# Order of the row gathers behind a router: the tiles of 128 of experts 0 and 1 ahead of the gathers of later experts

## The chip, the cores and the metric

One core of a Trainium2 chip. The metric is the time of one execution on the device in microseconds, as the median of several runs.

## The reference

Three stages run one after the other on 1536 tokens of width 512: an attention with a local window and block summaries, a layer of 8 experts of which each token uses at most one, and a dense network with a cosine. Only the second is touched by the change:

```python
skip_score = x @ w_skip
do_compute = skip_score > 0
xc = x[do_compute]
logits = xc @ w_gate
e_idx = np.argmax(logits, axis=1)
...
for e in range(E):                      # 8 experts, w1[e]: 512x1024, w2[e]: 1024x512
    mask = e_idx == e
    h = np.maximum(xc[mask] @ w1[e], 0.0)
    y[mask] = gate_w[mask, None] * (h @ w2[e])
out[do_compute] = xc + y
```

The third stage is `g = h * cos(h)` with `h = x @ w_in`, and `g @ w_out` (512 to 2048 and back).

## The kernel before, in words

**Stages.** The attention ends at about 85 us of the span and leaves all rows in a DRAM tensor xb. The router counts the tokens of each expert (CNT) and makes lists of row numbers: GIA for the first 32 tokens of each expert (64 half rows), GIS for up to 64 more, GIB for a full tile of 128 more. Which of the last two is used depends on the count: up to 32 tokens neither, up to 96 the 64 rows, above that the 128 rows (with the 64 again for what is left in some cases). The branches are real ones, evaluated by every engine from registers (`tc.If`, L941, L1169, L1171, L1173).

**Gathers.** Three helpers issue an indirect DMA each from GpSimd (all through L626): `ex_gather(e)` fetches the first rows of expert e into xg (e = 2 to 7; those of 0 and 1 are issued earlier, at L817 and L818), `ov_gather(e)` the 64 rows into xo, and `many_gather(e)` the 128 rows into xm, if the count asks for it. `many_gather` first loads two counts into registers on every engine. GpSimd issues in program order.

**The expert loop** (L1261 on). For expert e TensorE turns the hidden rows of e (`ex_t`), multiplies the rows of expert e + 1 with its first matrix (`ex_w1`, L642), turns the rows of expert e + 2 (`ex_x`, L604), and multiplies with the second matrix of e (`ex_w2`, L979). `ex_out` adds and scatters the rows (L630); a scatter into xb waits for the gathers that read xb before it. `overflow(e)` then turns the 64 rows (L995, 64x64), and if there are more, the 128 rows xm (L995, 128x128), and multiplies them with both matrices (`full_tile`, L1034, L1049, result at L1059). Between these the tables `WORK` and `START` put work of the next stage: conversions of w_in and w_out (raw loads L897, then L907 to L920) and the order of rows (L1065 on).

**Weights.** `load_piece` (L179) issues 512 KB of an expert's matrices from SyncE (SP); four pieces are one matrix, a unit, and eight units have buffers at a time. A piece waits for the gather that is handed to it (`after`), otherwise for the landing of the piece three ahead of it (`AHEAD`). Units 4 (expert 2's first matrix) and before are loaded during the attention; the pieces that the changed lines pace are those of units 5, 6 and 7, twelve in all. Units 8 to 15 are asked for at the end of each of the first four experts, when the buffers of that expert come free. SP also works in program order.

**The third stage** begins at about 223 us. It is a row of matmuls on TensorE (L1188, L1333, L1399), with the conversions beside them, and ends with scatters to the output.

Of the kernel before, what the change touches and what calls it, by code (L numbers as in the profile page):

```python
# [31 lines left out]
NE = 8  # L32
# [83 lines left out]
def tile_kernel(ctx: ExitStack, tc: tile.TileContext, consts, qh, kh, vh, vw, w9, w1, w2, w_in, w_out, out):  # L116
# [56 lines left out]
    def load_w(u):  # L173
        pool = ring[u % NU]
        wt[u] = pool.tile([P, 4096], F32, tag="w", name="w")
        for part in range(4):
            wq.append((u, part))

    def load_piece(after=None, half=None):  # L179

        if not wq:
            return
        u, part = wq.pop(0) if half != 0 else wq[0]
        e, kind = divmod(u, 2)
        k, w = (4, w1) if kind == 0 else (8, w2)
        ks, fs = slice(part * k // 4, (part + 1) * k // 4), slice(None)
        if half is not None and kind == 0:
            fs = slice(512 * half, 512 * half + 512)
        elif half is not None:
            ks = slice(2 * part + half, 2 * part + half + 1)  # L190
        d = nc.sync.dma_start(out=wt[u].rearrange("p (k f) -> p k f", k=k)[:, ks, fs],
                              in_=w[e].rearrange("(k p) f -> p k f", p=P)[:, ks, fs])
        if after is None and len(pieces) >= AHEAD:
            after = pieces[-AHEAD]
        if after is not None:
            tc.add_manual_dep(d.ins, after.ins.name, SYNC, reason="pace")
        pieces.append(d)
# [427 lines left out]
    def gather(dst, idx, src):  # L625
        return nc.gpsimd.indirect_dma_start(out=dst, out_offset=None, in_=src,  # L626
                                            in_offset=bass.IndirectOffsetOnAxis(ap=idx, axis=0))
# [10 lines left out]
    def ex_w1(e, ph, h):  # L638
        w, x = W1(e), xe.pop(e)
        for k in range(4):  # L640
            for c in range(4):
                nc.tensor.matmul(ph[CAP * c:CAP * c + CAP, :], x[:, QA * (k % 2) + CAP * (k // 2):][:, 0:CAP],  # L642
                                 w[:, k, 256 * c:256 * c + 256],
                                 start=(k == 0), stop=(k == 3), skip_group_check=True)
        nc.scalar.activation(out=h, in_=ph, func=AF.Relu)
        hs[e] = h
# [234 lines left out]
    def cv_alloc(q, half):  # L881
        if q == 2:
            WQ[q, half] = WQ[0, half]
        else:
            t = (wpb if q % 2 else wpa).tile([P, 2, 4, 512], F32R, tag="w", name="wx")
            WQ[q, half] = (t[:, 0], t[:, 1])
# [3 lines left out]
    def cv_load(q, i, after=None):  # L890
        kind, j = divmod(i, 4)
        r = cvt.tile([P, 1024], I32, tag="raw", name="raw", bufs=3 if q == 0 else 2)
        if kind == 0:
            src = w_in[j * P:(j + 1) * P, q * 512:(q + 1) * 512].bitcast(I32)
        else:
            src = w_out[(4 * q + j) * P:(4 * q + j + 1) * P, :].bitcast(I32)
        d = nc.sync.dma_start(out=r, in_=src)  # L897
        if after is not None:
            tc.add_manual_dep(d.ins, after.ins.name, SYNC, reason="rows first")
        raws[q, i] = r  # L900
# [23 lines left out]
    def ex_gather(e):  # L924
        xg.append(m1.tile([QA, 256], F32, name=f"xg{e}"))
        return gather(xg[e], GIA[:, e:e + 1], xb2)

    def ov_gather(e):

        xo[e] = ysrc[e] if e < 3 else xo[e - 1] if e == NE - 1 else m1.tile([P, DM], F32, name=f"xo{e}")  # L930
        return gather(half(e), GIS[:, e:e + 1], xb)

    def half(e):
        return xo[e][YT:P] if e == NE - 1 else xo[e][0:YT]
# [3 lines left out]
    def many_gather(e):  # L938
        cnts[e] = cnt(0, e, NTOK), nc.values_load(CNT[0:1, 2, e:e + 1], min_val=0, max_val=1, skip_runtime_bounds_check_because=why)
        xm[e] = m2.tile([P, DM], F32, tag="xm", name="xm")  # L940
        with tc.If(cnts[e][0] > CAP + YT):  # L941
            apart(gather(xm[e], GIB[:, e:e + 1], xb), None, ("m", e % 2))

    def ex_x(e):
        xe[e] = m2.tile([P, P], F32, tag="xe", name="xe")
        turn_x(xg[e], xe[e], ps_g, "g", nc.scalar.copy)
# [4 lines left out]
    def apart(d, to=None, key=None):  # L951

        for p, k in outs + inner:
            if key is None or k != key:
                tc.declare_no_dep(d.ins, p.ins, reason="every token has one slot of one expert")
        if to is not None:
            to.append((d, key))
        return d
# [4 lines left out]
    def ex_t(e):  # L963
        h = hs[e]
        pt = ps_l.tile([P, 2, P], F32, tag="p", name="pth")
        for s in range(2):
            nc.tensor.transpose(pt[:, s, :], h[:, s * P:(s + 1) * P], ident)
        hT = m2.tile([P, 2, P], F32, tag="hT", name="hT")
        nc.scalar.copy(out=hT, in_=pt)
        hs[e] = hT  # L970

    def ex_w2(e, hT, po, ns=range(8)):

        w = W2(e)
        for n in ns:
            c, s = divmod(n, 2)
            for a in range(2):
                o = QA * s + CAP * a
                nc.tensor.matmul(po[o:o + CAP, :], hT[:, s, CAP * c:CAP * c + CAP], w[:, n, 256 * a:256 * a + 256],  # L979
                                 start=(c == 0), stop=(c == 3), skip_group_check=True)  # L980

    def ex_out(e, po, yo=None):
        x = xg[e]
        if yo is None:
            yo = x
        for s in range(2):
            nc.vector.scalar_tensor_tensor(out=yo, in0=po[QA * s:QA * s + QA, :], scalar=GTA[:, e:e + 1], in1=yo if s else x,
                                           op0=ALU.mult, op1=ALU.add)
        d = scatter(xb2, SIA[:, e:e + 1], yo, 2 * NTOK)
        apart(d, outs, ("g", e))  # L990
# [134 lines left out]
    def cnt(k, e, top):  # L1125
        return nc.values_load(CNT[0:1, k, e:e + 1], min_val=0, max_val=top, skip_runtime_bounds_check_because=why)
# [38 lines left out]
    def overflow(e):  # L1165

        x, xb_ = xm.pop(e), half(e)
        n, part = cnts.pop(e)
        with tc.If(n > CAP):  # L1169
            xx = tile_x(xb_, YT, nc.vector.tensor_copy, YT if e == NE - 1 else 0)  # L1170
            with tc.If(n > CAP + YT):  # L1171
                full_tile(W1(e), W2(e), x, GTB[:, e:e + 1], SIB[:, e:e + 1], ("m", e % 2))
            with tc.If(part > 0):  # L1173
                part_tile(e, xb_, xx, GTS[:, e:e + 1], SIS[:, e:e + 1], ("o", e))
# [64 lines left out]
    def do(where, e):  # L1239
        for a in WORK.get(where + str(e), "").split():  # L1240
            kind = a.rstrip("0123456789")
            for i in a[len(kind):] or "0":
                acts[kind](int(i))
# [3 lines left out]
    load_w(7)  # L1247
    cv_load(0, 0, first_in)
    load_piece(first_in)
    for e in range(NE):  # L1250
        if e + 2 < NE:
            load_piece(ex_gather(e + 2))
        load_piece(ov_gather(e))
        if e == 0:
            many_gather(0)
        if e in (1, 3):
            cv_load(0, (e + 1) // 2)
    while wq:
        load_piece()
    do("S", 0)  # L1260
    for e in range(NE):  # L1261
        ex_t(e)
        do("T", e)
        if e + 1 < NE:
            ex_w1(e + 1, ps_h.tile([P, 256], F32, tag="h", name="ph"), m2.tile([P, 256], F32, tag="h", name="h"))
        if e + 2 < NE:
            ex_x(e + 2)
        do("B", e)
        if e + 1 < NE:
            many_gather(e + 1)  # L1270
        po = ps_o.tile([P, 256], F32, tag="o", name="po")
        ex_w2(e, hs.pop(e), po)
        ex_out(e, po)
        overflow(e)
        do("J", e)
        if e == 4:
            cv_alloc(0, 0)
            t = wpa.tile([P, 2, 4, 512], F32R, tag="w", name="yb")
            Y[0] = (t[:, 0], t[:, 1])
        if e == 5:  # L1280
            gs.append(wpa.tile([P, 2, 4, 512], F32R, tag="w", name="g0"))
            cv_alloc(0, 1)
        do("A", e)
        for u in range(2 * e + NU, min(2 * e + 2 + NU, 2 * NE)):
            load_w(u)
        while wq:
            load_piece()
        do("Z", e)
# [176 lines left out]
```

## Time and profile before

| what | value |
|---|---|
| median of 3 runs | 494.01 us (493.82 to 1119.29) |
| profiled execution | 495.81 us, of which the span from first to last instruction is 494.0 us |
| TensorE matmuls busy | 443.3 us, 90% |
| VectorE, ScalarE, GpSimd busy | 308.3, 213.7, 148.9 us |
| mean granted clock of TensorE | 0.960 |
| transfers | 76.09 MB, 154 GB/s over the span |

The page has one row of the granted clock and of the transfers for 40 equal slices of 12.35 us. It shows the clock at a half in the tenth slice, and 230 to 350 GB/s in the first sixteen slices, up to about 198 us, with little behind them. The share of busy time of an engine is a mean over the three stages, so the stretch of the experts, 85 to 223 us, has to be read by itself.

### The profile page before, as it was taken

How to read it: one execution, taken by the hardware profiler on the slowest of the kernel's cores; microseconds unless marked ns; L12 is line 12 of the kernel's file. 1: busy time of each engine (PE TensorE's matmuls, PEld its weight loads, DVE VectorE, ACT ScalarE, POOL GpSimd, SP SyncE). 2: the span in 40 equal slices, each digit the busy share in tenths (PEclk: the TensorE clock that was granted, in tenths of full speed). 3: DMA queues.
4: the chain of work that ended last, by engine and by line, in shares of the span. 5: the costliest groups of instructions: out<-in, count | busy, mean ns of one | idle time of the engine just before them, and what ended most of it. 6: DMA issues, size and time to landing. Idle time of an engine off the chain costs nothing.

```text
span 494.0 us, 8759 instructions
## 1 busy us (share of the span) xinstructions
PE 443.3 (90%) x3037; PEld 331.9 (67%) x3037; DVE 308.3 (62%) x862; ACT 213.7 (43%) x518; POOL 148.9 (30%) x156
## 2 busy tenths in 40 slices
PE   6999998950999886948999999999999999999994
PEld 3878886520444342526888888888888888888883
DVE  4798998640051141465658797999889965563741
ACT  2988885100231130332646566644536433150600
POOL 3576652372120026125115232223123200003033
PEclk9999999985899998997999999999999999999997
DMA  9998986779979897103501322322132000002021
GB/s 238 300 306 294 341 300 235 230 248 304 350 255 317 308 325 278 57 12 100 181 23 47 124 85 86 126 86 88 55 116 85 1 1 0 1 0 75 12 104 67
DMA packets 36785, 76.09 MB, mean 154 GB/s; under 512 B 4249, under 2 KB 12955, under 8 KB 36724
## 3 DMA queue, kind: packets, MB, share of 16 engines
q1 hardware_dynamic: 33476, 66.07, 41.2%
q0 software_dynamic: 3248, 9.27, 5.6%
q8 instruction: 31, 0.51, 0.4%
q14 instruction: 30, 0.25, 0.2%
HBM read 68.15 MB, written 7.60 MB: 153 GB/s over the span
## 4 chain that ended last, share of the span: by engine, by line
PE 29%; issue 18%; DVE 3%; POOL 3%; POOLq 0%; ACT 0%; DVEq 0%; ACTq 0%
PE pf L1188 15%; PE py L1333 11%; POOL out L630 2%; PE py L1399 2%; DVE g L1204 1%; PE pt L1118 1%; DVE cvu L911 0%; DVE cvc L912 0%; DVE u L1194 0%; DVE c L1198 0%; POOL wx L920 0%; POOLq L1461 0%; DVE nn L1193 0%; DVE cvu L909 0%; ACT u L1192 0%
## 5 line engine op out<-in xcount | busy, mean ns | idle before, releaser
L1188 PE MATMUL pf<-yb,wx 128*128 128x512 f32 x576 | 136.3, 394 | 6.6 <-DVEq L1157 4.8
L1188 PEld LDWEIGHTS pf<-yb,wx 128*128 128x128 f32 x576 | 109.1, 190 | 30.4 <-issue 7.8
L1333 PE MATMUL py<-wx,g 128*128 128x512 f32 (+1 forms) x540 | 121.6, 384 | 0.0
L1333 PEld LDWEIGHTS py<-wx,g 128*128 128x128 f32 x540 | 99.9, 188 | 20.2
L1192 ACT ACTIVATE u<-pf,qbias 128x512 f32<-128x512 f32 x46 | 31.5, 684 | 86.7 <-PE pf L1188 82.7
L920 POOL TENSOR_TENSOR wx<-cvc,wx 128x512 fp32r<-128x512 f32 x24 | 34.7, 1445 | 94.7 <-ACT wx L919 91.5
L1204 DVE TENSOR_TENSOR g<-c,g 128x512 fp32r<-128x512 f32 x42 | 42.6, 1015 | 0.8 <-ACT g L1203 0.7
L1339 DVE TENSOR_TENSOR ya<-py,ya 128x512 f32<-128x512 f32 (+1 forms) x37 | 23.8, 671 | 28.2 <-PE py L1333 28.2
L340 ACT ACTIVATE sm<-sm,nm 128x128 f32<-128x128 f32 x96 | 37.5, 393 | 5.6 <-DVE nm L328 5.5
L1193 DVE TENSOR_SCALAR nn<-u 128x512 f32<-128x512 f32 x46 | 19.5, 424 | 30.6 <-ACT u L1192 30.6
L1197 ACT ACTIVATE c<-u 128x512 f32<-128x512 f32 x46 | 28.8, 627 | 17.5 <-DVE g L1204 16.1
L630 POOL DMA_INDIRECT out<-ya,PERM x11 | 10.9, 990 | 79.9 <-DVE ya L1339 79.3
L1194 DVE TENSOR_TENSOR u<-u,nn 128x512 f32<-128x512 f32 x46 | 31.9, 693 | 1.6
L1198 DVE TENSOR_TENSOR c<-pf,c 128x512 f32<-128x512 f32 x46 | 31.5, 684 | 0.9 <-ACT c L1197 0.7
L322 PE MATMUL ps<-kT,qbd 128*128 128x128 f32 x192 | 28.1, 296 | 3.3 <-DMA qbd<-qh 3.3
L350 POOL TENSOR_TENSOR sm<-sm,su 128x512 f32<-128x512 f32 x23 | 23.9, 1040 | 21.5 <-DVE su L349 10.8
L322 PEld LDWEIGHTS ps<-kT,qbd 128*128 128x128 f32 x192 | 26.1, 209 | 4.3 <-issue 4.1
L1203 ACT CAST g<-c 128x512 fp32r<-128x512 f32 x46 | 28.0, 608 | 1.0 <-DVE c L1198 1.0
L1059 DVE SCALAR_TENSOR_TENSOR xm<-pox,GTB,xm 128x512 f32<-128x512 f32 x2 | 1.5, 750 | 42.9 <-PE pox L1049 42.9
L328 DVE CUSTOM_DVE_ANT_0 sm<-ps,cst 128x128 f32<-128x128 f32 x96 | 23.7, 284 | 6.1 <-PE ps L322 6.1
L919 ACT CAST wx<-cvc 128x512 fp32r<-128x512 f32 x24 | 14.9, 622 | 16.4 <-DVE cvc L912 16.4
L979 PE MATMUL po<-w,hT 128*32 128x256 f32 x256 | 18.0, 429 | 3.5 <-ACTq L1169 1.9
(250 smaller groups left out, 631.5 us busy)
## 6 DMA issues: line engine op xcount, KB each, us to landing
w<-w SPq DMA_DIRECT2D x62, 512.0 KB, 5.9
raw<-w_in SPq DMA_DIRECT2D x16, 512.0 KB, 3.9
raw<-w_out SPq DMA_DIRECT2D x16, 512.0 KB, 3.3
kT<-kh SPq DMA_DIRECT2D x8, 384.0 KB, 6.5
vn<-vh SPq DMA_DIRECT2D x12, 256.0 KB, 5.2
xb<-xtok SPq DMA_DIRECT2D x12, 256.0 KB, 4.3
qd<-qh SPq DMA_DIRECT2D x4, 512.0 KB, 5.2
vt<-vw SPq DMA_DIRECT2D x12, 128.0 KB, 4.8
```

Source lines behind the costliest of these rows:

```text
L322: nc.tensor.matmul(ps[:, p, :], q[:, p, :, :].rearrange("p h (a t) -> p (h a) t", t=2)[:, :, t % 2], kT[b][:, p, k0:k0 + P], start=True, s ...
L340: nc.scalar.activation(out=sm[:, p, :], in_=sm[:, p, :], func=AF.Exp, scale=-1.0, bias=nm[:, p:p + 1], accum_out=su[:, p:p + 1])
L350: nc.gpsimd.tensor_tensor(out=sm, in0=sm, in1=su.unsqueeze(2).to_broadcast([P, NP, P]), op=ALU.mult)
L920: eng.tensor_tensor(out=lo, in0=c, in1=hi.bitcast(F32), op=ALU.subtract)
L1188: nc.tensor.matmul(p, w[:, k, fs], y[:, k, :], start=(n == 0), stop=(n == 11))
L1192: nc.scalar.activation(out=u, in_=p, func=AF.Identity, scale=1.0 / (2.0 * math.pi), bias=qbias)
L1194: nc.vector.tensor_tensor(out=u, in0=u, in1=nn, op=ALU.subtract)
L1197: nc.scalar.activation(out=c, in_=u, func=AF.Sin, scale=TWO_PI)
L1198: nc.vector.tensor_tensor(out=c, in0=p, in1=c, op=ALU.mult)
L1203: nc.scalar.copy(out=gh, in_=g)
L1204: (nc.gpsimd if i in POOL_G else nc.vector).tensor_tensor(out=gl, in0=g, in1=gh.bitcast(F32), op=ALU.subtract)
L1333: nc.tensor.matmul(p, a[:, ws], b[:, f, cs], start=(n == 0), stop=(n == 11))
```

## The change

The loop that issues the gathers is written in another order, and the call for the 128 rows of expert 1 moves from the expert loop to it. Nothing is added or left out.

```diff
     load_w(6)
     load_w(7)
     cv_load(0, 0, first_in)
     load_piece(first_in)
-    for e in range(NE):
-        if e + 2 < NE:
-            load_piece(ex_gather(e + 2))
+    for e in range(2, 5):
+        load_piece(ex_gather(e))
+    for e in range(2):
+        many_gather(e)
         load_piece(ov_gather(e))
-        if e == 0:
-            many_gather(0)
-        if e in (1, 3):
-            cv_load(0, (e + 1) // 2)
+    for e in range(2, NE):
+        if e + 3 < NE:
+            load_piece(ex_gather(e + 3))
+        load_piece(ov_gather(e))
+        if e in (3, 5):
+            cv_load(0, (e - 1) // 2)
     while wq:
         load_piece()
...
         do("B", e)
-        if e + 1 < NE:
+        if 0 < e < NE - 1:
             many_gather(e + 1)
```

On GpSimd, before, the gathers behind the routing end like this; xo5 and xo6 are rows of 64 of experts 5 to 7, xm_2049 is the tile of 128 of expert 1, and the scatter is expert 0's result:

```order
L626 DMA xg7_1975<-xb_68,GIA_1006 64x256
L626 DMA xo5_1978<-xb_68,GIS_1010 64x512
L626 DMA xo6_1980<-xb_68,GIS_1010 64x512 x2
L1126 TENSOR_LOAD CNT_83
L939 TENSOR_LOAD CNT_83
L941 COMPARE_AND_BRANCH
L626 DMA xm_2049<-xb_68,GIB_1008 128x512
L941 UNCONDITIONAL_BRANCH
L941 ISA
L941 UNCONDITIONAL_BRANCH
L630 DMA xb_68<-xg0_1691,SIA_1007 3072x256
```

With the change the same queue reads like this from the first xo on; xm_1969 is now the tile of expert 1, and xg3, xg4 and the tile of expert 0 stand ahead of these rows:

```order
L626 DMA xo0_1919<-xb_68,GIS_1010 64x512
L1126 TENSOR_LOAD CNT_83
L939 TENSOR_LOAD CNT_83
L941 COMPARE_AND_BRANCH
L626 DMA xm_1969<-xb_68,GIB_1008 128x512
L941 UNCONDITIONAL_BRANCH
L941 ISA
L941 UNCONDITIONAL_BRANCH
L626 DMA xo1_1920<-xb_68,GIS_1010 64x512
L626 DMA xg5_1974<-xb_68,GIA_1006 64x256
L626 DMA xo2_1921<-xb_68,GIS_1010 64x512
```

The gather of expert 1's 128 rows has moved from the end of the row to the place behind the first xo, and ten gathers follow it now.

On TensorE the register loads and the branch of that gather move from expert 0's second matrix (L979) to a place ahead of the matmul for the order of rows (L1065). These are the two pieces of the difference:

```order
 L941 COMPARE_AND_BRANCH
 L941 UNCONDITIONAL_BRANCH x2
+L1126 TENSOR_LOAD CNT
+L939 TENSOR_LOAD CNT
+L941 COMPARE_AND_BRANCH
+L941 UNCONDITIONAL_BRANCH x2
 L1065 LDWEIGHTS ones
 L1065 MATMUL pd<-ado,ones 128x13
```

The second piece stands 16 matmuls further on, and xg_1927 in it is expert 2's first rows:

```order
 L642 MATMUL ph<-w,cst 32x256 x16
 L604 MATMUL ptx<-ident,xg_1927 128x64 x2
-L1126 TENSOR_LOAD CNT
-L939 TENSOR_LOAD CNT
-L941 COMPARE_AND_BRANCH
-L941 UNCONDITIONAL_BRANCH x2
 L979 MATMUL po<-w,hT 32x256 x16
 L1169 COMPARE_AND_BRANCH
```

The loads of expert 2's gather, which stand at the same place one expert later, stay where they were.

On SyncE the pieces of weights keep their order, and the second and third raw loads move behind pieces of unit 7. The queue now ends like this ahead of the expert loop (128x1024 is a piece of unit 6, 128x2x512 of unit 7):

```order
L191 DMA w<-w 128x1024
L1126 TENSOR_LOAD CNT
L939 TENSOR_LOAD CNT
L941 COMPARE_AND_BRANCH
L941 UNCONDITIONAL_BRANCH x2
L191 DMA w<-w 128x1024 x3
L191 DMA w<-w 128x2x512 x2
L897 DMA raw<-w_in 128x1024
L191 DMA w<-w 128x2x512 x2
L897 DMA raw<-w_in 128x1024
```

Before, one raw load stood ahead of the last three pieces of unit 6 and the other ahead of the last three of unit 7; the pieces are now handed the gathers in the order xg2, xg3, xg4, xo0, xo1, xg5, xo2, xg6, xo3, xg7, xo4.

## Rows read from the trace of the kernel before

**Rows 1.** The chain that ended last, its first piece (start us, us, what).

```profile
222.91 1.19 PE pf L1188 x2
```

**Rows 2.** Engines by stretch: us, busy of PE, PEld, DVE, ACT, POOL, then PEclk, DMA.

```profile
core 0: us, PE busy (x) PEld busy (x) DVE busy (x) ACT busy (x) POOL busy (x), PEclk, DMA share, GB/s
223.00:494.00 271.00, 262.03 (x1172) 216.98 (x1172) 194.04 (x304) 119.66 (x209) 62.29 (x50) 0.98 0.20 67
...
109.00:122.00 13.00, 0.04 (x1) 0.00 (x0) 0.89 (x2) 0.00 (x0) 4.26 (x5) 0.50 0.99 287
...
92.00:104.00 12.00, 9.70 (x162) 5.28 (x158) 7.72 (x44) 2.32 (x7) 4.73 (x6) 1.00 0.63 196
...
140.00:150.00 10.00, 8.85 (x96) 4.56 (x95) 8.14 (x19) 1.50 (x4) 3.70 (x5) 1.00 0.72 239
150.00:166.00 16.00, 16.00 (x51) 6.43 (x49) 0.92 (x2) 2.37 (x4) 1.94 (x2) 1.00 0.94 315
```

**Rows 3.** TensorE in order of time: start, us, instruction, idle time before it and releaser.

```profile
104.31 0.31 PE L604 MATMUL ptx<-ident,xg 64*128 64x64 f32 x2 [2.04 <-DMA xg<-xb,GIA]
105.61 2.82 PE L979 MATMUL po<-w,hT 128*32 128x256 f32 x32 [0.99 <-ACT xe L605]
108.35 0.69 PE L995 MATMUL ptx<-ident,xo 64*128 64x64 f32 x4
122.06 1.09 PE L995 MATMUL ptx<-ident,xm 128*128 128x128 f32 x4 [13.02 <-DMA xm<-xb,GIB]
...
145.97 0.66 PE L995 MATMUL ptx<-ident,xm 128*128 128x128 f32 x4
```

**Rows 4.** GpSimd in order of time, 84 to 132 us.

```profile
97.08 0.90 POOL L626 DMA_INDIRECT xo<-xb,GIS  x1 [5.54 <-DVE GIS L860]
98.95 0.90 POOL L626 DMA_INDIRECT xg<-xb,GIA  x1 [0.97 <-remote]
...
113.52 0.97 POOL L626 DMA_INDIRECT xm<-xb,GIB  x1 [0.30 <-issue]
122.79 0.95 POOL L630 DMA_INDIRECT xb<-xg,SIA  x1 [8.31 <-DMA xm<-xb,GIB]
124.93 0.97 POOL L626 DMA_INDIRECT xm<-xb,GIB  x1 [1.19 <-issue]
```

**Rows 5.** Tiles: xo from 96 to 114 us (first row), then xm in all.

```profile
DMA to landing us min/median/max: 4.4/7.8/8.7
...
L1059 DVE SCALAR_TENSOR_TENSOR xm<-pox,GTB,xm x2: 750/750/751, 140.5 to 162.5; 128x512 f32<-128x512 f32 x2
...
DMA to landing us min/median/max: 3.4/4.6/8.4
```

**Rows 6.** Weight pieces (L191) by window: twelve, eight, eight, sixteen of them.

```profile
L191 SPq DMA_DIRECT2D w<-w x12: 328/372/1602, 93.7 to 116.4; - x12
...
DMA to landing us min/median/max: 3.9/11.5/14.0
...
L191 SPq DMA_DIRECT2D w<-w x8: 328/356/379, 126.8 to 138.3; - x8
...
L191 SPq DMA_DIRECT2D w<-w x8: 328/378/450, 145.4 to 160.1; - x8
...
L191 SPq DMA_DIRECT2D w<-w x16: 328/368/424, 166.1 to 192.1; - x16
```

**Rows 7.** TensorE at experts 5 and 7; DMA queue q8 from 101 to 104.

```profile
182.32 1.91 PE L642 MATMUL ph<-w,xe 128*32 128x256 f32 x27
186.92 0.63 PE L642 MATMUL ph<-w,xe 128*32 128x256 f32 x5 [2.68 <-issue]
...
216.18 1.93 PE L979 MATMUL po<-w,hT 128*32 128x256 f32 x32 [1.89 <-ACTq L1169]
...
q8 instruction: 1, 0.02, 2.2%
```

**Rows 8.** ScalarE in order of time, 122 to 148 us.

```profile
136.76 1.76 ACT L907 ACTIVATE C<-raw 128x512 f32<-128x512 f32 x3
141.75 0.37 ACT L969 COPY hT<-pth 128x256 f32<-128x256 f32 x1 [3.22 <-PE pth L967]
```

## The prediction

> **What bounds the kernel now.** I read three views in this order. First the chain of waits that ended last. It can be followed back no further than 222.91 us, to the first matmul of the second network that has both its operands [rows 1], and from there on TensorE is busy for 262.03 of 271 us [rows 2]. That stretch is more than half of the span, and the change touches none of it: it can only begin sooner. Second the table by stretches of the part before it. [...] Third TensorE's timeline around it: the matmuls that turn the 128 gathered rows of expert 1 (xm) start at 122.06 after 13.02 us of waiting for the gather; a little earlier stand two smaller waits, 2.04 us for the gather of xg3 and 0.99 us ahead of the second matrix of expert 1 [rows 3]. GpSimd's timeline tells why: the gather of xm is issued at 113.52, as the last one of a row of gathers that began at 97.08, one each 1.21 us ((113.52 - 98.95) / 12), and every other gather of that row lands before anything needs it [rows 4]. Expert 0 has no such tile, since there are only two xm gathers; the second, at 124.93, is expert 2's.
>
> **The change, part by part.** The order of work moves on three queues.
>
> *GpSimd.* xg3 and xg4 now follow xg2 at once, in the hole in which GpSimd waits for the indices GIS until 97.08 [rows 4]. They are issued at about 92 and 93 and, with the 4.4 to 8.7 us that gathers took there [rows 5], xg3 lands by 101; TensorE comes to it at 102.3 (104.31 - 2.04), so the 2.04 us go. Behind ov0 (97.08 + 0.90) comes expert 1's xm gather, at about 98.4, and ov1 at 99.7. What lands then, and when? The gathers of 64 rows took 4.4 to 8.7 us, median 7.8, xm took at most 8.4 [rows 5]. So xm is there by 106.8 and ov1 between 104.1 and 108.4; I take the median, 107.5.
>
> *TensorE.* The two register loads and the branch of expert 1's gather move ahead of the matmul of the order of rows. The same three instructions cost 0.99 us at 105.61, where nothing was queued ahead of them [rows 3]; I charge 0.99 at the new place and strike it at 105.61, where the sequencer no longer stops at xg3 and can run ahead. TensorE is then ready for expert 1's rows at 108.35 - 2.04 - 0.99 + 0.99 = 106.3, waits to 107.5 for ov1, and begins on xm 0.7 us later, at 108.2 instead of 122.06. Gain 13.9 us, with bounds of 15.0 (only TensorE decides, 107.0) and 13.0 (ov1 at 8.7).
>
> [...]
>
> *The clock.* The tile of expert 1 took from 122.06 to 140.5, expert 2's from 145.97 to 162.5 [rows 3, 5]: 18.4 against 16.5 us for the same instructions, and the first begins at the half clock that the idle stretch left behind [rows 2]. Without those idle 13 us the clock need not fall. I take 1.5 of these 1.9 us (bounds 0 and 1.9).
>
> *The weights on SyncE.* SP issues in order, and each of twelve pieces (512 KB) waits for one gather. Two of them (those behind xg3 and xg4) now start between 96 and 101 instead of after 104, into 92:104, where the DMA share is only 0.63 [rows 2]. They take 1.05 MB off the full stretch that follows, 3.3 us of it at the 315 GB/s of 150:166 [rows 2]. The row of twelve ended near 130 (116.4 + 13.5, just under the longest landing of 14.0 [rows 6]); now near 126.8. But these two pieces also run beside the xm gather; rival 2 gives what that may cost. [...]
>
> TensorE needs expert 6's first matrix at 182.32 [rows 7], then at about 167.4 (15 us less). From the end of the twelve to it lie 23 transfers of 512 KB: five matrices of four pieces (those of experts 4 and 5 and the first of expert 6) and three raw loads of the second network's weights. At 1.64 us each (eight from 126.8 to 138.3) they are there at 164.5, at 1.73 (sixteen from 166.1 to 192.1) at 166.6 [rows 6]; the gap of 140:150, share 0.72 [rows 2], closes because expert 1's buffers come free sooner. I take 0.5 us of cost. The other end is 2.1 us each, the pace of 145.4 to 160.1 [rows 6], 175.1 and 7.7 us.
>
> *ScalarE and the second xm.* The third raw load now stands behind the twelve pieces, so it lands at about 127. ScalarE comes to these conversions at about 122 (136.76 less 15), and behind them, in its order, stands the copy of hT for expert 2, due at 126.8 (141.75 less 15) [rows 8]: it may be held to 127.5 or a little longer. TensorE's matmuls with expert 3's first matrix, which come before hT is read, cover part of that. I charge 0.5 (0 to 3). Expert 2's xm gather follows the first scatter, which waits for all gathers: the last is now issued at 98.4 + 10 x 1.21 = 110.5, landed by 119.2, the scatter follows, the gather 2.14 us behind that (124.93 - 122.79), and it lands at most 8.4 later, at 130.1 [rows 4, 5]; TensorE wants it at 145.97 - 15 = 131. Nothing.
>
> **The sum.** 13.9 + 1.5 - 0.5 - 0.5 = 14.4 us. The profiled execution took 495.81 with a span of 494.0; it becomes 481.4. The median of the runs is 494.01, 1.8 less than the profiled one, so 479.6. The likeliest case alone ranges from 477.1 (15.0 + 1.9) to 484 (13.0 less 3).
>
> **The rivals.**
> 1. *The weights become the bound.* At 2.1 us a piece expert 6's matrix lands at 175.1, the gain shrinks to 182.32 - 175.1 = 7.2, time 486.8. For it: a DMA share of 0.94 to 0.99 in the full stretches [rows 2]. Against it: the paces of 1.64 and 1.73 before and after that stretch [rows 6]. Chance 0.13.
> 2. *The gather lands late.* With 14.0 us like the slowest weight piece ov1 lands at 113.7, the tile starts at 114.4, 7.7 us sooner, with the clock down as before: 486.3. For it: the pieces moved ahead of it. Against it: no gather took over 8.7, though some ran in the fullest stretch. Chance 0.09.
> 3. *The change doesn't do what it says*: the xm gather, though written earlier, waits for its buffer or indices until near its old time; 494. Its row of before shows only 0.30 us of idle time ahead of it, with no release named, so nothing is known to hold it [rows 4]. Chance 0.05.
> 4. *Slower.* All weights still to come get slower because they now run beside TensorE's work and the gathers without a pause. Expert 7's second matrix is needed at 216.18 [rows 7] and ends 35 transfers after 126.8. From (216.2 - 126.8) / 35 = 2.55 us a piece the whole gain is gone; at 2.8 it lands at 224.8, 8.6 late: 502.6. The slowest pace in the rows is 2.1, and that for eight pieces only [rows 6]. Chance 0.04.
>
> **How the numbers follow.** The forecast has 0.69. Two per cent, about what a measurement of this kernel can tell from no change, is 9.9 us, that is 484.1. Forecast plus the early edges of rivals 1 and 2 (0.03 each, where pace or landing lie half way) make 0.75 for faster; the rest of those two, rival 3 and the mild part of rival 4 make 0.22; slower by over 2% keeps 0.03. The range runs from 476.0, a little under the best bounds, to 488.0, which takes in rivals 1 and 2.
>
> **What would show it.** In the changed profile the matmuls on xm start between 107 and 109 and wait for xo or nothing; GpSimd issues xm near 98.4; the granted clock stays at the upper level through expert 1; the chain's first matmul of the second network moves from 222.9 to about 208.5. If TensorE waits around 165 to 175 for expert 6's weights, rival 1 is right; if xm or ov1 land after 110, rival 2. I am wrong if the stretch from 109 to 122 is still empty, or if the time comes back as waits between 125 and 205.

## The result, and the profile after

The changed kernel took 480.57 us (median of five executions, 479.55 to 482.83) beside 494.01 us for the kernel before: ratio 0.9717, 95% interval 0.9685 to 0.9749. The profiled execution took 482.83 us with a span of 481.0; it is the slowest of the five. That is close to the forecast of 479.6, but the later experiments put a limit on it: in the two later series that ran the same kernel again, on two chips, it took 499 us. Ratios leave out slow executions: of those told of here, 1119.29 us of the kernel before in this measurement and 502.18 us of it in the third series.

First TensorE's timeline of the changed kernel, for the stretch of [rows 3] (start, us, engine, line, instruction, operands, count, idle time before it and what ended it):

```profile
97.53 0.18 PE L1065 MATMUL pd<-ado,ones 128*128 128x13 bf16 x1 [1.51 <-issue]
...
104.39 0.33 PE L604 MATMUL ptx<-ident,xg 64*128 64x64 f32 x2
104.65 1.49 PE L979 MATMUL po<-w,hT 128*32 128x256 f32 x20
108.01 1.06 PE L979 MATMUL po<-w,hT 128*32 128x256 f32 x12 [1.87 <-issue]
110.22 0.54 PE L995 MATMUL ptx<-ident,xo 64*128 64x64 f32 x4 [1.15 <-DVE xg L987]
110.69 1.11 PE L995 MATMUL ptx<-ident,xm 128*128 128x128 f32 x4
...
130.36 0.46 PE L1095 MATMUL ptt<-oi,OR 128*128 128x24 bf16 x12 [0.42 <-PEq L1173]
...
135.41 0.66 PE L995 MATMUL ptx<-ident,xm 128*128 128x128 f32 x4
```

The wait of 13.02 us for xm is gone, and so is that of 2.04 us for xg3 at the matmuls of L604. The first matmul on xm starts at 110.69 instead of 122.06. Two smaller waits are new: 1.87 us with no release to name in the middle of expert 1's second matrix (x20, then x12 of its 32 matmuls), and 1.15 us ahead of the matmuls on xo, which the row puts down to VectorE's addition (L987); what it really waited for comes out of a later trace, and is told in the part on the prediction. The tile of expert 1 ends with the matmul at L1095: 19.67 us after it began. In the trace of before that row stood at 140.92, 18.86 us after 122.06.

GpSimd in order of time, for [rows 4]:

```profile
98.15 0.90 POOL L626 DMA_INDIRECT xo<-xb,GIS  x1 [2.98 <-DVE GIS L860]
99.38 0.97 POOL L626 DMA_INDIRECT xm<-xb,GIB  x1 [0.33 <-issue]
100.65 0.91 POOL L626 DMA_INDIRECT xo<-xb,GIS  x1 [0.30 <-issue]
...
109.99 0.90 POOL L626 DMA_INDIRECT xo<-xb,GIS  x1 [1.16 <-DMA xm<-xb,GIB]
...
124.03 0.97 POOL L626 DMA_INDIRECT xm<-xb,GIB  x1 [1.18 <-PE pgx L1042]
```

xm is issued right behind the first xo. The fourth row is of use beyond its own engine: a later gather waited until xm had landed, so xm landed at about 109.99, some 10.6 us after its issue.

The table by stretches, for [rows 2] (us, busy time of PE, PEld, DVE, ACT and POOL with counts, granted clock, DMA share, GB/s):

```profile
92.00:104.00 12.00, 9.95 (x171) 5.83 (x172) 7.00 (x42) 2.20 (x7) 7.15 (x8) 1.00 0.90 284
...
110.00:126.00 16.00, 15.05 (x40) 7.20 (x41) 0.54 (x2) 4.15 (x6) 4.63 (x5) 0.79 1.02 305
...
140.00:150.00 10.00, 10.00 (x30) 4.51 (x29) 0.00 (x0) 2.37 (x4) 0.93 (x1) 1.00 1.03 398
...
210.00:481.00 271.00, 261.85 (x1172) 216.93 (x1172) 194.10 (x304) 119.71 (x209) 62.29 (x50) 0.98 0.20 67
```

The transfers fill the holes that they had in 92:104 (share 0.90, before 0.63) and 140:150 (1.03, before 0.72). The stretch of expert 1 still has a granted clock below the upper level (0.79). The last 271 us are the same work as before, begun 12.9 us sooner (210.05 against 222.91).

Last, TensorE at experts 5 and 7 and at the start of the third stage, for [rows 7] and [rows 1]:

```profile
171.81 1.92 PE L642 MATMUL ph<-w,xe 128*32 128x256 f32 x26
174.47 0.63 PE L642 MATMUL ph<-w,xe 128*32 128x256 f32 x6 [0.74 <-issue]
175.93 1.93 PE L979 MATMUL po<-w,hT 128*32 128x256 f32 x32 [0.57 <-ACT xe L605]
179.53 3.65 PE L1006 MATMUL phy<-w,xx 128*64 128x512 f32 x16 [1.28 <-DVEq L1171]
...
202.03 3.19 PE L979 MATMUL po<-w,hT 128*32 128x256 f32 x32 [1.88 <-ACTq L1169]
210.05 0.76 PE L1188 MATMUL pf<-yb,wx 128*128 128x512 f32 x1 [4.83 <-DVEq L1157]
```

The same matmuls of expert 5 in the kernel before, which [rows 7] does not have:

```profile
188.39 3.61 PE L979 MATMUL po<-w,hT 128*32 128x256 f32 x32 [0.58 <-ACT xe L605]
193.68 3.65 PE L1006 MATMUL phy<-w,xx 128*64 128x512 f32 x16 [1.29 <-DVEq L1171]
```

So the gain can be followed by place. At xm it is 11.37 us (122.06 - 110.69), at the end of that tile 10.56 (140.92 - 130.36). At expert 5 it grows to 14.15 (193.68 - 179.53): the wait with no release is 0.74 instead of 2.68 us, and the 32 matmuls behind it take 1.93 instead of 3.61 us. At expert 7 it is still 14.15 (216.18 - 202.03), and there it loses 1.26 again, since these matmuls now take 3.19 instead of 1.93. What is left is 12.86 us at the start of the third stage, and 13.0 in the span. This compares one trace of each kernel; the second series has another trace of the kernel before, and it shows that the 3.6 us at expert 5 are not the change's.

### The profile page after: what moved, and what is told of

Same layout as the page of the kernel before. It is cut to its first block, busy times and chain, and to the rows that moved or that the text cites. A ratio compares the mean times of both kernels' runs of the same rounds, so it can differ in the third digit from the quotient of the medians.

```text
span 481.0 us, 8758 instructions
## 1 busy us (share of the span) xinstructions
PE 442.9 (92%) x3035; PEld 331.4 (69%) x3037; DVE 309.2 (64%) x862; ACT 213.7 (44%) x518; POOL 148.4 (31%) x156
## 4 chain that ended last, share of the span: by engine, by line
PE 30%; issue 19%; DVE 3%; POOL 3%; POOLq 0%; ACT 0%; DVEq 0%; ACTq 0%
PE pf L1188 16%; PE py L1336 11%; POOL out L630 2%; PE py L1402 2%; DVE g L1204 1%; PE pt L1118 1%; DVE cvu L911 0%; DVE cvc L912 0%; DVE u L1194 0%; DVE c L1198 0%; POOL wx L920 0%; POOLq L1464 0%; DVE nn L1193 0%; DVE cvu L909 0%; ACT u L1192 0%
## 5 line engine op out<-in xcount | busy, mean ns | idle before, releaser
L979 PE MATMUL po<-w,hT 128*32 128x256 f32 x256 | 17.3, 405 | 4.3 <-ACTq L1169 1.9
```

## The first series: which part of the change does it

Four kernels ran on one chip, beside the kernel before, which took 494.8 us there. The changed kernel itself did not run in this series, so what is compared with it below is compared with the first measurement.

**Expert 1's rows alone ahead.** From the kernel before, with only the call for xm moved up:

```diff
+        if e == 0:
+            many_gather(1)
...
-        if e + 1 < NE:
+        if 0 < e < NE - 1:
             many_gather(e + 1)
```

> Only the 128-row gather of expert 1 is moved up, behind xo0; xg3 and xg4 stay behind it. My theory (the gain is the end of the 13.0 us wait for xm): xm is issued near 99 and lands by 110; xg3 is issued near 100 and TensorE waits 2 to 5 us for it near 103; the matmuls on xm start at 110 to 112 instead of 122.1, and the time is 481 to 485. Rival (the early xg3 and xg4, and with them the two early weight pieces, carry most of the gain): 488 or more.

It took 483.28 us (480.85 to 485.13), ratio 0.9765, interval 0.9706 to 0.9824. The xm rows are there in time: their matmuls start at 110.31 and the tile takes 16.91 us. The two small waits ahead of it stay (2.08 and 1.09 us).

**Only the gathers of xg3 and xg4 ahead.** The loop of the change, with expert 1's rows left where they were:

```diff
+    for e in range(2, 5):
+        load_piece(ex_gather(e))
+    for e in range(2):
...
+        load_piece(ov_gather(e))
```

> Only xg3 and xg4 are moved up into the hole ahead of GIS; the 128-row gather of expert 1 stays the last of the row. My theory: xm is issued near 112 and lands at 119 to 121, so TensorE still waits some 11 us; 490 to 493. Rival (the two early weight pieces carry most of the gain): 484 to 487.

It took 493.55 us (489.78 to 496.48), ratio 0.9968, interval 0.9930 to 1.0006. TensorE's wait for xm remained:

```profile
119.34 1.09 PE L995 MATMUL ptx<-ident,xm 128*128 128x128 f32 x4 [11.85 <-DMA xm<-xb,GIB]
```

Of the two parts, then, the move of xm carries nearly all: 11.5 us of it alone against 1.3 us for the other, the second within what the measurement leaves open (its interval takes in 1).

**The two weight pieces later.** The changed kernel, with no weight piece handed to the gathers of xg3 and xg4:

```diff
-    for e in range(2, 5):
-        load_piece(ex_gather(e))
+    load_piece(ex_gather(2))
+    for e in range(3, 5):
+        ex_gather(e)
```

> The gathers stand as in the change, but no weight piece is handed to xg3 and xg4, so two pieces fewer run beside xm and xo1. In the change xm took about 10.5 us to land, above the 8.4 that I used. Theory A (those two pieces slow it): xm and xo1 land within 9 us, the matmuls on xm start 1 to 2 us sooner than in the change (110.7), and the time is 478 to 480.5. Theory B (the gathers queued behind it slow it): landing and start stay within 0.5 us, time within 1 us of the change (480.6) or a little longer, as weights come later.

It took 479.06 us (477.82 to 480.83), ratio 0.9668, interval 0.9620 to 0.9716. The first row is from the view of the tile xm, the others are TensorE's:

```profile
DMA to landing us min/median/max: 5.4/5.4/5.4
...
108.23 0.66 PE L995 MATMUL ptx<-ident,xm 128*128 128x128 f32 x4
...
125.14 0.47 PE L1095 MATMUL ptt<-oi,OR 128*128 128x24 bf16 x12 [0.42 <-PEq L1173]
...
169.61 0.64 PE L642 MATMUL ph<-w,xe 128*32 128x256 f32 x8 [1.05 <-DMA w<-w]
172.05 0.64 PE L642 MATMUL ph<-w,xe 128*32 128x256 f32 x8 [1.80 <-DMA w<-w]
```

Without the two pieces beside it the gather of xm lands after 5.4 us, not 10.6 (one trace of each), and the tile takes 16.91 us (125.14 - 108.23), not 19.67. TensorE is 5.2 us ahead of the changed kernel at the end of that tile (130.36 - 125.14). But the third stage of this trace begins only 2.2 us sooner (207.86 against 210.05): now the pieces of expert 6's first matrix land too late, 1.05 and 1.80 us of waiting. That is where the next bound lies.

**xm ahead of everything.** The changed kernel, with the rows of experts 0 and 1 asked for right behind xg2:

```diff
+    load_piece(ex_gather(2))
+    many_gather(0)
+    many_gather(1)
+    for e in range(3, 5):
...
-        many_gather(e)
```

> The 128-row gather of expert 1 moves further up, ahead of xg3 and xg4 into the hole before GIS. It is issued near 94 and lands by 102, long before use. If xm's own late landing decided the start in the change, the matmuls on xm now start 1 to 2 us sooner and the time is 478 to 480. If xo1 (64 rows) lands at the same late moment, nothing moves: 480 to 481. If the clock stays up through expert 1's tile because TensorE no longer idles ahead of it, another 2.5 us come off: 476 to 478.

It took 480.47 us (479.07 to 480.85), ratio 0.9699, interval 0.9653 to 0.9744.

```profile
108.31 1.06 PE L979 MATMUL po<-w,hT 128*32 128x256 f32 x12 [1.52 <-issue]
...
109.68 0.66 PE L995 MATMUL ptx<-ident,xm 128*128 128x128 f32 x4
...
126.58 0.47 PE L1095 MATMUL ptt<-oi,OR 128*128 128x24 bf16 x12 [0.42 <-PEq L1173]
```

xm was issued at 93.9 and landed 5.2 us later, ten microseconds before its use. The median gains nothing by that: what starts the tile here is TensorE itself, after 1.52 us without a release. The tile takes 16.90 us, as in the kernel above, and the third stage of this trace begins at 207.59, 2.5 us ahead of the changed kernel's trace. The further 2.5 us that were expected of a clock that stays up do not show in the median, so the changed kernel's trace, its slowest execution, is probably not like the other four; no run shows it.

## The second series: the gain is not there

The unaltered kernels ran once more on another chip, and with them two that leave out code whose branches always skip it with this input, and these branches: of `overflow(e)` only the calls for experts 1, 2 and 5 remain.

```diff
-        overflow(e)
+        if e in (1, 2, 5):
+            overflow(e)
```

> The changed kernel once more, unaltered, for a second trace. In its first trace the clock fell to the lower level at 110.4 for 6.8 us and expert 1's tile took 19.7 us, while three variants that keep the clock up there took 16.9. If that fall belongs to the change, it comes again and the tile takes 18.5 us or more. If it is one execution's (that run, 482.8, was the slowest of five), the tile takes about 17 us and the span is 478 to 479.5.

> The kernel before once more, unaltered. In its first trace TensorE stood 2.7 us inside expert 6's first matrix (near 184 to 187) and ran at the lower clock for 3.4 us after it; the change had 0.7 us there and no fall, 3.6 us of its gain. If this is a property of the kernel before, both come again (idle 2 us or more, second-matrix matmuls 3 us or more). If it is one execution's, they differ by more than a microsecond.

> The change without the code of the overflow blocks of experts 0, 3, 4, 6 and 7, which these inputs never enter (their branches always skip it); nothing that is executed is left out but these branches. Theory A (the stalls with no release named, 1.9 us near 106, 0.7 near 174 and 1.9 near 202, are instruction fetches after the taken branches): they shrink to under 0.5 us each, and the time is 475 to 478.5. Theory B (they come from something else, such as the full transfers): they stay within 0.5 us and the time is 479.5 to 481.

> The kernel before without the same never-entered blocks. Theory A: the 2.7 us near 185 and the lower clock after it go, and the 1.9 us near 216; the 2.0 us wait for xg3 and the 13.0 us wait for xm stay; 488 to 490.5. Theory B: 493 to 495.

The kernel before took 494.01 us here too (13 executions), and 495.36 in the profiled execution. The changed kernel took 499.43 in its only execution. Without the skipped code it took 491.14 us (488.20 to 493.35), ratio 0.9956, interval 0.9924 to 0.9987; the kernel before without it took 487.27 (486.46 to 489.59), ratio 0.9860, interval 0.9827 to 0.9894. For the changed kernel both theories missed (475 to 481 expected), since its own time was no longer 480. For the kernel before the theory that the waits come from something else (493 to 495) falls, and the time is a little under the 488 to 490.5 of the other. Without the skipped code the new order is the slower one here too, by 3.9 us (491.14 - 487.27).

The two repeated traces answer what they were taken for in part. Expert 1's tile of the changed kernel now takes 16.90 us (142.81 - 125.91) and not 19.67, but TensorE came to it in another way, so this does not settle why it was slow. And the kernel before has 1.30 us of wait at expert 5 instead of 2.68, with 1.93 us for the matmuls behind it instead of 3.61 (rows below): the 3.6 us there belong to its first trace and not to the change.

Here is TensorE of the kernel before in this series, from 108 us on:

```profile
109.58 0.24 PE L604 MATMUL ptx<-ident,xg 64*128 64x64 f32 x1 [0.32 <-issue]
111.74 0.38 PE L979 MATMUL po<-w,hT 128*32 128x256 f32 x1 [1.91 <-issue]
...
120.87 0.58 PE L979 MATMUL po<-w,hT 128*32 128x256 f32 x1 [0.82 <-issue]
122.28 3.57 PE L979 MATMUL po<-w,hT 128*32 128x256 f32 x26 [0.83 <-issue]
...
126.62 0.63 PE L995 MATMUL ptx<-ident,xm 128*128 128x128 f32 x4 [0.23 <-DMA xm<-xb,GIB]
```

Six matmuls of expert 1's second matrix come one by one, with 0.8 to 1.9 us of idle time before each and no release named. In this kernel that is nearly free: TensorE would have stood waiting for xm in that stretch anyway, and the wait of 13.02 us has shrunk to 0.23. The tile starts 4.6 us later, but the gather of xm was issued 4.9 us later as well (118.45 against 113.52). In the changed kernel nothing stands there to hide it.

## The third series: the square of order and skipped code

The unaltered changed kernel was timed on a third chip, with both orders without the skipped code, and with the later weights joined to it.

> The changed kernel, unaltered, timed in rounds beside the kernel before. In the single look at it in the second series TensorE got its instructions between 104 and 117 us one about every 0.7 us, xm's first matmul came at 125.9 us and the profiled execution took 499.4 us; in the first trace that stretch was one stall of 1.87 us and the execution 482.8 us. Theory A (the trickle belongs to the conditions of that series, as all four traces of it had one, with the kernel before among them): here every execution lies on one side, 479 to 484 us without a trickle, or 495 to 500 us with one, and the trace shows which. Theory B (it comes and goes from one execution to the next): the executions of this run spread over 480 to 499 us.

> The changed kernel with no code for the spill-over blocks of the experts that have none with this input (0, 3, 4, 6 and 7), on the same chip as the unaltered one. Theory A (skipped code costs TensorE a wait for instructions where a jump passes it; the two such waits near 174 and 185 us go, with the half clock behind them): 4 to 8 us under the unaltered changed kernel, 473 to 478 us where that has 480. Theory B (waits of this kind lie beside weights that are late anyway): within 2 us of it.

> The kernel before with the same code left out: the fourth corner of the square of order by skipped code. Theory A: 6 to 8 us under the kernel before, as 487.3 against 494.0 us in the second series, and the gain of the new order is then about the same with and without the skipped code, 11 to 15 us, where no trickle of instructions covers it. Theory B (in the kernel before the wait for xm hides what the skipped code costs at expert 1, so that leaving it out is worth more behind the new order): the gain of the new order is 2 us or more larger without the skipped code.

> The changed kernel with both edits that stood to gain: no weight pieces issued between the gathers for experts 3 and 4, and no code for the spill-over blocks that stay empty. Sum of the two where they do not meet: 1.5 us for the pieces (479.06 against 480.57 us) and 4 to 8 us for the code, so 471 to 475 us. Theory that they meet (with both, TensorE reaches expert 5 and 6 earlier than unit 12's weights land, which kept the run with later weights waiting 1.05 and 1.80 us there): 475 to 478 us, with TensorE waiting for weights between 160 and 172 us in the trace.

| third chip, us | with the skipped code | without it |
|---|---|---|
| order of before | 494.57 (490.90 to 502.18) | 487.20 (486.39 to 488.18) |
| order of the change | 499.04 (495.20 to 501.62) | 491.60 (489.33 to 495.13) |

The changed kernel's ratio here is 1.0108, interval 1.0029 to 1.0187. On this chip the new order costs 4.5 us with the skipped code (499.04 - 494.57) and 4.4 without it (491.60 - 487.20); leaving out the skipped code gains 7.4 us in either order. The loss of the new order is under two per cent, with an interval clear of 1. So the theory that the skipped code is worth more behind the new order falls, and so does the one that unlike conditions come and go between executions: none of the four executions of the changed kernel was near 480 (495.20 to 501.62). The kernel with both edits took 490.89 us (489.05 to 495.59), ratio 0.9936, interval 0.9892 to 0.9979, far over the 471 to 478 that either theory gave it.

TensorE of the unaltered changed kernel in this series:

```profile
102.62 1.19 PE L979 MATMUL po<-w,hT 128*32 128x256 f32 x15
104.14 0.38 PE L979 MATMUL po<-w,hT 128*32 128x256 f32 x1 [0.33 <-issue]
...
107.75 0.38 PE L979 MATMUL po<-w,hT 128*32 128x256 f32 x1 [1.02 <-issue]
108.46 0.38 PE L979 MATMUL po<-w,hT 128*32 128x256 f32 x1 [0.33 <-issue]
109.18 0.62 PE L979 MATMUL po<-w,hT 128*32 128x256 f32 x1 [0.35 <-issue]
110.59 1.35 PE L979 MATMUL po<-w,hT 128*32 128x256 f32 x2 [0.79 <-issue]
113.41 1.01 PE L979 MATMUL po<-w,hT 128*32 128x256 f32 x2 [1.48 <-issue]
...
117.64 1.08 PE L979 MATMUL po<-w,hT 128*32 128x256 f32 x3 [0.81 <-issue]
...
126.35 0.66 PE L995 MATMUL ptx<-ident,xm 128*128 128x128 f32 x4
```

The starts lie 0.71, 0.72, 1.41 and 2.82 us apart: always about 0.7 us or a multiple of it. Fifteen matmuls of L979 took 1.19 us; the other seventeen of that block took until 118.7. xm had been issued at 101.89 and nobody waits for it; the tile starts at 126.35, where the kernel before has 126.62 in the second series. SyncE goes by the same steps: in the second series' trace of the changed kernel its issues start at 110.02, 111.45, 112.86, 114.28, 115.68 and 117.10 us. ScalarE is held up too: the result that its L645 reads was complete at 102.42 (100.49 + 1.93), and L645 began at 116.28. GpSimd is not; its gathers keep their 1.21 us, and VectorE's eight instructions of 104:110 took 1.66 us, 0.21 each, as the six of L1089 did in the first trace of the kernel before (1.27 us). First ScalarE's row, then GpSimd's:

```profile
116.28 0.38 ACT L645 ACTIVATE h<-ph 128x256 f32<-128x256 f32 x1 [14.80 <-remote]
```

```profile
100.65 0.90 POOL L626 DMA_INDIRECT xo<-xb,GIS  x1 [4.19 <-DVE GIS L860]
101.89 0.97 POOL L626 DMA_INDIRECT xm<-xb,GIB  x1 [0.34 <-issue]
...
114.10 0.91 POOL L626 DMA_INDIRECT xo<-xb,GIS  x1 [0.30 <-issue]
```

All eight traces of the second and third series have such a stretch, of 11 to 16 us; the six others (the kernel before and the changed one in the first measurement, and the four of the first series) have none. It goes with the row of gathers: it begins only after the first xo is issued, and its last step comes 3.5 to 4.0 us after the last gather of the row, in all eight, though that gather is issued anywhere from 113.50 to 118.45 (here 117.64 - 114.10 = 3.5). The steps are not fetches of instructions, one each: from 105 to 119 this trace has no packet on an instruction queue. The stretch is also poor in records: from 104 to 116 the trace holds 38 records of landings, for 3.1 MB moved, where the first trace of the same kernel holds 186 for 2.7 MB. So the recording of the profile suffers there, or even causes the steps; whether executions without a profile have them, no run shows.

Nor does this trace hold the loss. It took 495.20 us, the least of the four, and its third stage begins at 222.42, where the kernel before has 223.04 in the second series: the stretch accounts for the gain that is gone, and not for the 4.5 us. With three traces of the new order without the skipped code goes another wait, earlier, in which ScalarE takes 3.9 to 4.3 us to begin on TensorE's first result of this stage. In the third series' kernel:

```profile
93.09 0.31 PE L604 MATMUL ptx<-ident,xg 64*128 64x64 f32 x2 [0.44 <-DMA xg<-xb,GIA]
97.29 3.64 PE L642 MATMUL ph<-w,cst 128*32 128x256 f32 x32 [3.90 <-ACT cst L605]
```

In the three traces of the old order from these two chips it is at most 1.4 us. Five gathers run at that place in the new order, three in the old one. That fits the 4.4 us by which the new order is slower without the skipped code, but with it (1.4 and 0.3 us in its two traces) it explains nothing, and the 4.5 us there stay unexplained.

What the skipped code costs can be read at expert 5. The first rows are the kernel before in the second series, the other two the same without the skipped code in the third:

```profile
185.37 1.91 PE L642 MATMUL ph<-w,xe 128*32 128x256 f32 x27
188.59 0.63 PE L642 MATMUL ph<-w,xe 128*32 128x256 f32 x5 [1.30 <-issue]
...
190.08 1.93 PE L979 MATMUL po<-w,hT 128*32 128x256 f32 x32 [0.60 <-ACT xe L605]
```

```profile
182.28 1.93 PE L642 MATMUL ph<-w,xe 128*32 128x256 f32 x32
...
211.33 1.93 PE L979 MATMUL po<-w,hT 128*32 128x256 f32 x32 [2.06 <-ACT hT L969]
```

The wait with no release is gone and the 32 matmuls run as one; the wait at expert 7 stays (2.06 us; 1.89 in [rows 7]), now with ScalarE's copy as its releaser. From the end of expert 1's tile to the third stage it is 75.84 us (217.38 - 141.54) instead of 79.54 (223.04 - 143.50); on the chip of the second series the kernel without it has 75.90 there (218.02 - 142.12). The rest of the 7.4 us lies before and behind that.

## Why the prediction was right, and where it was not

**What bounds the kernel: right.** The wait for xm was TensorE's own, the third stage only had to begin sooner, and in the first measurement it did: 210.05, by the span 13.0 of the 14.4 us predicted. The move of xm alone gave 11.5 us in the first series. One slip stands in the step: not every other gather of the row lands in time, as its own 2.04 us for xg3 show.

**xm is there by 106.8: wrong by its size.** It was issued at 99.38, one microsecond behind the 98.4 of the step, so rival 3 falls. For the landing the step took the slowest gather of [rows 5], 8.4 us, as the upper end. Measured: 10.6. What the step left to rival 2, the two weight pieces beside the gather, is the cause as far as single traces show it: without them it is 5.4.

**xo of expert 1 decides the start, at 107.5: right in kind, 2.6 us too early.** TensorE was through with the second matrix at 109.07 (108.01 + 1.06) and waited 1.15 us more. The row names VectorE's addition (L987). But with xm ahead of everything the same matmul began at 109.29, while that addition ran until 110.41, so it does not need it. What it does wait for is xo: the last landing recorded for that gather is at 110.08, 9.4 us after its issue at 100.65, where the step took 7.8 and allowed 8.7.

**TensorE ready at 106.3: 2.8 us too early.** About 1.1 of these are no effect of the change: TensorE was later by that much at 92.28 already (91.18 before), ahead of every moved instruction. The register loads cost what was charged (1.51 less the 0.39 us that this matmul waited before, so 1.12, for 0.99). The rest is the new wait of 1.87 us; in this trace it cost little, as xo was not there. The wait for xg3 (2.04 us) went and one without a release came, of nearly its size, 20 matmuls behind the branch, and a packet of the instruction queue q8 begins just ahead of it. In the three traces that have the wait it ends 2.7 to 2.8 us after that packet begins (105.19 to 108.01, 103.25 to 105.93 with only xg3 and xg4 ahead, 105.54 to 108.31 with xm first). With the later weights the packet begins at 104.02, TensorE comes to that place later, and does not wait. Whether the packet makes the wait, no run shows. The step gave 13.9 us of gain at this place; it was 11.37.

**The clock, 1.5 us: wrong in sign for the profiled execution, and its cause not shown.** The tile took 19.67 us, 0.8 more than before, with a granted clock of 0.79 in 110:126; in the three kernels of the first series that do without the long wait it took 16.9, that is 2.0 us less than before (granted clock 1.00 in 104:126 with xm alone ahead, and in 108:125 with the later weights). So a tile at the upper level is worth the 1.5 us of the step and a little more, but the step's reason, the long idle stretch, does not tell when the tile gets it. Already in the trace of before the clock fell ahead of the long wait: the matmuls at 105.61 took 2.82 us [rows 3], with a granted clock of 0.72 in 105:108.5, against 1.93 for expert 7's 32 [rows 7] at 1.00 in 216:218.2. Nor does TensorE's work ahead of the tile tell: from 103 to 110 it was 4.20 of 7 us in the changed kernel, and 5.48 and 6.08 with xm first and with the later weights, but only 3.82 with xm alone ahead, where the tile took 16.91 us all the same (the row has the busy times in the order of [rows 2]):

```profile
103.00:110.00 7.00, 3.82 (x67) 2.06 (x59) 2.36 (x10) 0.77 (x3) 5.19 (x6) 1.00 0.82 244
```

**The weights and ScalarE, 0.5 us of cost each: none in the result.** Expert 2's second matrix follows at once (133.15, no wait), and so do its xm matmuls (135.41). Rival 1 was close all the same: 2 to 5 us further ahead, TensorE does wait for expert 6's first matrix (1.05 + 1.80 us with the later weights).

**Experts 5 and 7: not in the sum.** 3.6 us more and 1.3 us less, from a wait that got shorter and the clock behind it (at expert 5 granted 1.00 in 175.9:177.9, before 0.55 in 188.3:192.1; at expert 7 0.58 in 202:205.3, before 1.00 in 216:218.2); on balance they filled the gap that the steps above had left (10.56 + 3.59 - 1.29 = 12.86). The second trace of the kernel before has neither the long wait nor the slow matmuls at expert 5, so in the comparison of the two traces it was luck that the total came out right with its terms for the start and for the clock wrong.

**What failed altogether: that one trace speaks for the chip.** Rival 4 was the slower side, with every weight piece at 2.55 us or more. The slower side did come, on two chips, by what no rival named: in the traces the gain goes in a stretch in which several engines get along by steps of 0.7 us while the gathers run, and some 4 us more are lost that the traces do not place. In the kernel before the 13 us of waiting lie in just that stretch, so its time is the same with that stretch and without it (494.0, 494.8, 494.0 and 494.6 us) and could not tell of it.

**What stays open.** What serves TensorE, ScalarE and SyncE every 0.7 us in that stretch, whether the recording of the profile has a part in it, whether it is the chip or the time of the series that has it, and whether fewer gathers at a time would end it: this was not tried. Nor is it shown what the other 4 us are by which the new order is slower on the third chip, nor why the clock fell in the first trace of the changed kernel (0.50 in 110.4:117.2).

## What to carry to other kernels

Where TensorE waits long for one transfer that stands last in a queue, moving it up can gain nearly the whole wait (here 11.5 us of 13.0), and the rest of the reordering hardly matters (1.3 us on the one chip that had both). What is asked for beside the moved transfer counts: in single traces it took 10.6 us with two weight pieces and 5.4 without, and holding them back only moved the wait to the weights of expert 6 (1.05 + 1.80 us). And a wait of 13 us hides what else is slow in its stretch, so a change that takes it away should be timed on more than one chip before it is kept: this one gained 13 us in the first measurement and lost 4 in the third series. A second trace of either kernel is worth as much: here it took 3.6 us out of a gain that seemed to be placed to the last microsecond.

## What the runs showed that was not expected

One gather of 128 rows took 5.2, 5.4, 8.4 or 10.6 us, with different transfers beside it. Code of blocks that are jumped over, with its branches, cost 7 us of 494 in this kernel (487.2 and 487.3 without it); the traces place about half of it, behind expert 1's tile. And in its traces the same program goes by steps of 0.7 us for 11 to 16 us in two series and at full pace in others, with the same total time for the kernel before.
